# Retention and SoLU layer on one core: keys and values of later steps in blocks of half a chunk, and new orders

## The chip, the core and the metric

The kernel runs on one core of a Trainium2 chip. The core has five engines with queues of their own: PE multiplies matrices, DVE and POOL work on vectors, ACT applies functions and copies, SP only issues transfers (DMAs), which 16 DMA engines carry out. Each engine works through its instructions in the order in which the program puts them; semaphores make one wait for another. The metric is the time of one execution on the device in microseconds. A median of three runs is given, and a profile of one further execution.

## What is computed

Eight heads of a causal attention with a decay per head, for 8 sequences of 576 positions, and then a layer over all 4608 tokens:

```python
scores = scale * np.matmul(q, k.transpose(0, 1, 3, 2))
gamma = 1.0 - 2.0 ** (-5.0 - np.arange(H, dtype=np.float32))
Dmat = np.where(rel >= 0, gamma[:, None, None] ** rel[None, :, :], 0.0)
x = np.matmul(scores * Dmat[None, :, :, :], v)        # then heads side by side: 4608 x 512
...
h = x @ w_in                                           # 4608 x 1024
e = np.exp(h - h_max)
solu = h * e / (np.sum(e, axis=-1, keepdims=True) + 1e-09)
ln = (solu - mu) / np.sqrt(var + 1e-06) * g_ln
out = ln @ w_out                                       # 4608 x 512
```

All inputs and the output are 32-bit floats.

## The kernel before

**Steps.** The sequences are cut into windows of 256 positions (two a sequence) and a rest of 64; the rests of four sequences make one more window. That gives 18 windows, and each is done in two steps of four heads: 36 steps i for the attention, and 36 tiles t of 128 tokens for the layer. Steps 16, 17, 34 and 35 are the windows made of rests (here: short windows), the other 32 are full. A full window is two chunks of 128 positions. Inside a chunk all pairs of query and key are computed and masked; what lies before the chunk comes from a state (the sum of k times v so far), which is carried on.

**Interleaving.** q, k and v are loaded so that partition p holds positions 2p and 2p + 1 of the window (line 380), which makes each run in DRAM 2 x 64 floats, 512 bytes. The two positions are the two "blocks" j of 64 keys a chunk. Because the blocks interleave, each of them meets all 128 queries of its chunk, and the mask has 256 columns for a pair of blocks.

**The named operations.** A planner (`plan`, line 122) lists them, and `emit` turns each into instructions. For step i:

- ldq, ldk, ldv (line 379; 384 for short windows, as four DMAs): loads, issued by SP, each into one of five buffers of its kind
- sq, sk, cv (lines 394 and 399): scaling of q and k by powers of the decay and the cast of v to 16 bits, mostly on POOL, one tile of 128 x 512 each
- T (lines 419 and 429): transposes of q and k on PE; Te or TL (455, 457): their copy out of PSUM on ACT
- K (533): k times v for the state on PE; st (554 to 557, DVE), sm (562, POOL) and sc (571, POOL) carry the state on
- S (508): 16 score matmuls of 64 x 128 on PE; mask (540): multiplication with the mask on DVE
- I (496): the state's share of the output on PE; V (521): masked scores times v, 16 matmuls of 64 x 128 on PE; xe (576): cast of the result into xT on ACT

For tile t: M1 (587, PE), ex (595, ACT), so (605 or 610, DVE), bnA and bnB (616, DVE) or va (624, ACT), fx and rs (633, ACT; 648 and 650, POOL), L (439 or 446, PE) with Le or TL, M2 (660, PE), oe (669, ACT), and out (680, or 685 for short windows), the store, issued by SP from one of three o_sb buffers. wi, wg, wc, WM, lwi and lwo prepare the weights once, at the start; PE also multiplies zeros there where it would stand idle (846).

**Order.** Each engine's order is fixed when the program is built. For the first steps and the last ones the orders are written out by hand as lists of names (FIRST and LAST, lines 42 to 95); between them an operation's place follows from a period of 4.92 us a step and an offset of its kind (the `key`), so that every step there repeats the one before. On PE a step in the middle reads M1, M2, I, L, T, V, K, S. SP issues the loads about five steps ahead, with the store of a finished tile after every third load. `order_ops` (line 233) plays the orders through with the durations of `DUR`, which settles only how the engines' lists are merged into one program and how many multiplications of zeros are put in.

Of the kernel before, what the change touches and what calls it, by code (L numbers as in the profile page):

```python
# [9 lines left out]
FP = mybir.dt.float32  # L10
# [3 lines left out]
P = 128  # L14
# [3 lines left out]
for _b in range(0, B, 4):  # L18
# [5 lines left out]
    T=0.26, L=0.26, Tw=0.45, Lw=0.45, I=0.22, V=0.23, K=0.13, S=0.22, M1=1.73, M2=1.73, M2h=0.87, oeh=0.42, G=0.1, WM=1.73,  # L24
    TL=1.03, Te=0.58, Le=0.58, xe=0.74, ex=1.22, oe=0.69, va=1.25, wiA=0.62, wiB=0.45, wg=0.68, wgD=0.43,
    cvA=0.62, mask=1.22, st=0.58, so=1.22, soA=1.3, bnA=0.68, bnB=0.89, fx=0.2, fin=0.42, wc=0.74, wm=0.62,
    sqD=0.75, gc=0.17, cvD=0.45, sq=1.04, sk=1.04, cv=0.61, sm=0.42, sc=0.81, rs=0.69, rsB=1.0,
    ldx=0.88, ldw=1.36, out=0.65,
)
HOP, PE_OUT = 0.07, 0.2  # L30
# [4 lines left out]
ON = {'sq0': 'DVE', 'sq1': 'DVE', 'cv0': 'ACT', 'cv1': 'ACT', 'sk2': 'DVE', 'sk3': 'DVE', 'cv2': 'ACT', 'cv3': 'ACT', 'cv4': 'ACT', 'cv5': 'ACT', 'cv6': 'ACT', 'cv7': 'ACT'}  # L35
CAP = dict(
    rawq=5, rawk=5, rawv=5, q16=3, k16=4, v16=4, ev=8, s=1, ret=2, xy=1, gg=6, gt=2, s160=4, s161=9, h=1,
    e=2, solu=4, osb=3, tl=1, tlx=2, tlT=1, tlL=1, wst=5,
# [3 lines left out]
FIRST = dict(  # L42
    PE=(
# [5 lines left out]
    ),  # L49
    ACT=(  # L50
# [4 lines left out]
    ),  # L55
    DVE=(
# [5 lines left out]
    ),  # L62
    POOL=(
# [4 lines left out]
    ),  # L68
    SP=(
# [5 lines left out]
    ),  # L75
)
LAST = dict(
    PE=(
        "I34 L30 V34 S35 M1_32 I35 L31 V35 M2_28 M1_33 M2_29 M2_31 M1_34 L32 M2_30 L33 L34 M1_35 M2_32 M2_33 "
        "L35 cs M2_34 M2_35 M3"  # L80
    ),
    ACT=(
        "oe27 xe34 ex32 Le30 Le31 oe28 xe35 ex33 fx15 oe29 ex34 Le32 oe30 Le33 oe31 fx16 ex35 oe32 Le34 oe33 "
        "Le35 fx17 oe34 oe35 oz"
    ),
    DVE=(
        "so31 mask35 bnA31 so32 bnB31 bnA32 so33 bnB32 so34 bnA34 bnA33 bnB33 bnB34 cnt so35 bnA35 ci bnB35"
    ),
    POOL=(
        "rs15 rs16 rs17"  # L90
    ),
    SP=(
        "out27 out28 out29 out30 out31 out32 out33 out34 out35"
# [11 lines left out]
def ev_T(i):  # L105
    return f"Te{i}" if i < NJ + 2 else f"TL{i - 2}"


def ev_L(t):
    return f"Le{t}" if t < NJ - 4 or t + 4 > NS - 3 else f"TL{t + 4}"  # L110

# [5 lines left out]
def wide(name):  # L117

    return name[0] == "T" and int(name[1:]) < NJ + 2 or name[0] == "L" and int(name[1:]) < NJ - 4


def plan():
    ops = []
    rank = {n: x - 1e4 for lst in FIRST.values() for x, n in enumerate(lst.split())}
    rank.update({n: x + 1e4 for lst in LAST.values() for x, n in enumerate(lst.split())})

# [5 lines left out]
    for i in range(NS):  # L132
# [3 lines left out]
        n = i - 2  # L136
        for x, (nm, cs) in enumerate((("q", "sq"), ("k", "sk"), ("v", "cv"))):
            op(f"ld{nm}{i}", "SP", 0.47 if full else 1.8, [], (i - 3 - CAP["rawq"], 1.5 + x), [("raw" + nm, [f"{cs}{i}"])], DUR["ldx"])
        op(f"sq{i}", "POOL", dict(POOL="sq", DVE="sqD"), [f"ldq{i}"], (i - 3, 0.5), [("q16", [f"T{i}"])])
        op(f"sk{i}", "POOL", dict(POOL="sk", DVE="sqD"), [f"ldk{i}"], (i - 3, 1.55), [("k16", [f"T{i}", f"K{i}" if full else ""])])  # L140
# [12 lines left out]
        jn = i >= NJ + 2  # L153
        op(f"T{i}", "PE", "T" if jn else "Tw", [f"sq{i}", f"sk{i}", f"L{i - 6}" if jn else ""], (n, 0.4), [] if jn else [("tlT", [f"Te{i}"])])
        if jn:
            op(f"TL{n}", "ACT", "TL", [f"T{i}", f"L{i - 6}"], (n, 1.0), [("ev", [f"I{i}", f"S{i}", f"M2_{i - 6}"])])
        else:
            op(f"Te{i}", "ACT", "Te", [f"T{i}"], (n, 1.0), [("ev", [f"I{i}", f"S{i}"])])
        op(f"S{i}", "PE", "S", [ev_T(i)], (i - 1, 0.95), [("s", [f"mask{i}"])])
        op(f"mask{i}", "DVE", "mask", [f"S{i}"], (i - 1, 1.6), [("ret", [f"V{i}"])])  # L160
        kv = i + 2 < NS and i + 2 >= NK and WINS[(i + 2) // 2][1] < 2
        op(f"I{i}", "PE", "I", sdep + [ev_T(i)], (i - 1, 4.75), [("xy", [f"xe{i}", f"st{i + 2}" if kv else ""])])
        op(f"V{i}", "PE", "V", [f"I{i}", f"mask{i}", f"cv{i}"], (i, 0.6))
        op(f"xe{i}", "ACT", "xe", [f"V{i}", f"K{i + 2}" if kv else ""], (i, 2.0))
    for t in range(NT):
# [5 lines left out]
        op(f"so{t}", "DVE", "soA" if va else "so", [f"ex{t}"], (m, 4.56), [("solu", [f"L{t}", f"va{t}" if va else f"bnB{t}"])])  # L171
# [5 lines left out]
        if c:  # L177
# [6 lines left out]
        after = [f"Te{NJ + 1}", f"Le{t - 1}"] if t == NJ - 4 else [f"TL{NS - 3}"] if t + 4 == NS - 2 else []  # L184
        after += [f"Le{t - 2}"] if t - 2 >= NS - 6 else []
        op(f"L{t}", "PE", "Lw" if early else "L", [f"so{t}"] + after, (m + 2, 0.1),
           [("tlL" if early else "tl" if jn else "tlx", [ev_L(t)])])
        if not jn:
# [3 lines left out]
        op(f"M2_{t}", "PE", "M2h" if end else "M2", need, (t + LAG, 3.1), [("h" if end else "xy" if late(t) and t % 2 else "s", [f"oe{t}"])])  # L192
# [5 lines left out]
    for c in range(4):  # L198
        op(f"lwi{c}", "SP", 0.47, [], (-4, 0.5 + 0.1 * c), [("wst", [f"wi{c}a", f"wi{c}b"])], DUR["ldw"])
        op(f"wi{c}a", "ACT", dict(ACT="wiA", DVE="wiB"), [f"lwi{c}"], (1, 0.1 * c))  # L200
        op(f"wi{c}b", "DVE", dict(ACT="wiA", DVE="wiB"), [f"lwi{c}"], (1, 0.1 * c))
    for c in range(0, 8, 2):
        op(f"lwo{c}", "SP", 0.47, [], (-2, 0.6 + 0.1 * c), [("wst", [f"wc{c}", f"wc{c + 1}"])], DUR["ldw"])
        for x in (c, c + 1):
            op(f"wg{x}", "DVE" if x % 2 else "ACT", dict(DVE="wgD", ACT="wg"), [f"lwo{c}", "gc"], (1, 1.0 + 0.1 * x))
            op(f"wc{x}", "DVE", "wc", ["wm" if WE else "WM", f"lwo{c}"], (4, 0.1 * x))
    op("G", "PE", "G", [], (-9999, 0.0), [("h", ["gc"])])
# [15 lines left out]
def parts(name):  # L223

    if name[:2] == "lw":
        return 1
    n = int(name[3:])
    if WINS[n // 2][1] == 2:
        return 2 if name[:3] == "out" else 4
# [731 lines left out]
```

## Time and profile before

| | us |
|---|---|
| median of 3 runs | 212.61 |
| lowest, highest | 212.51, 213.25 |
| span of the profiled execution (its own time: first to last instruction) | 210.9 |

The span is what the views of the profile cover; the runs also hold what lies around it. Other groups of the page that matter for the change, with count, total and mean:

| group | count | total us | mean ns |
|---|---|---|---|
| S, PE L508, 64 x 128 | 576 | 14.8 | 218 |
| V, PE L472 from ret and v, 64 x 128 | 576 | 14.7 | 217 |
| sq, POOL L394 | 34 | 35.4 | 1042 |
| M1, PE L587 | 288 | 68.5 | 380 |
| M2, PE L660, 128 x 512 | 280 | 65.8 | 379 |

How to read it: a group's total is the time in which at least one of its instructions ran; matmuls overlap, so the mean of one is longer than the distance from one to the next. "Idle before, releaser" says how long the engine stood before these instructions and what ended it. DMA issues are not counted as busy time of an engine: to see how full SP's queue is one has to take its timeline.

### The profile page before, as it was taken

The page shows a single profiled execution, that of the slowest core. Times are in us where ns is not written, and L with a number is a line of the kernel's source. Part 1 is how long each engine was busy: PE and PEld are TensorE (multiplying, and loading weights), DVE is VectorE, ACT ScalarE, POOL GpSimd, SP SyncE. Part 2 cuts the span into 40 slices and gives each one's busy share as a digit, 9 for nine tenths or more (in the row PEclk, how much of TensorE's full clock was granted, in tenths as well). Part 3 has the DMA queues.
Part 4 walks back from the last instruction along what each step waited for, and adds up shares of the span by engine and source line. Part 5 has one row for each costly group of instructions (what it writes and reads, how often), then busy time and mean ns, then how long its engine had stood idle before and what let it go on. Part 6 is the DMA issues. An engine that isn't in the chain of part 4 may idle for free. (4 is left out here: it accounts for less than half of the span.)

```text
span 210.9 us, 10171 instructions
## 1 busy us (share of the span) xinstructions
PE 200.8 (95%) x4400; PEld 113.2 (54%) x4400; DVE 166.1 (79%) x279; ACT 141.7 (67%) x235; POOL 141.7 (67%) x240
## 2 busy tenths in 40 slices
PE   7986989999999999999999999999999999999992
PEld 2442654665566555555555555555666555554451
DVE  6565779997868898978898898889988998753760
ACT  2375787897666776776666777666767777573752
POOL 7434758999997975948787979797979792001110
PEclk9999999999999999999999999999999999999999
DMA  5999999999666559778999686776355222311224
GB/s 157 345 355 334 329 311 269 301 293 306 195 188 188 169 139 278 217 214 259 314 288 305 198 252 183 217 234 181 94 152 153 54 57 67 71 63 54 101 101 104
DMA packets 64814, 42.66 MB, mean 202 GB/s; under 512 B 3320, under 2 KB 58624, under 8 KB 64768
## 3 DMA queue, kind: packets, MB, share of 16 engines
q1 hardware_dynamic: 64528, 41.82, 68.4%
q8 instruction: 34, 0.56, 1.2%
q10 hardware_dynamic: 240, 0.18, 0.5%
q14 instruction: 12, 0.10, 0.2%
HBM read 32.55 MB, written 9.44 MB: 199 GB/s over the span
## 5 line engine op out<-in xcount | busy, mean ns | idle before, releaser
L587 PE MATMUL h_ps<-w_in,xT 128*128 128x512 f16 x288 | 68.5, 380 | 0.0
L660 PE MATMUL o_ps<-w2c,ev 128*128 128x512 f16 (+1 forms) x296 | 67.6, 373 | 0.0
L610 DVE TENSOR_TENSOR solu<-h_ps,e_sb 128x1024 f16<-128x1024 f32 x32 | 39.2, 1223 | 16.7 <-ACT e_sb L595 16.5
L595 ACT ACTIVATE e_sb<-h_ps 128x1024 f32<-128x1024 f32 x36 | 36.8, 1023 | 21.9 <-PE h_ps L587 20.4
L540 DVE TENSOR_TENSOR ret<-s_ps,masks 128x1024 f16<-128x1024 f32 x36 | 43.9, 1220 | 6.0 <-PE s_ps L508 5.4
L660 PEld LDWEIGHTS <-ev 128*128 128x128 f16 x296 | 28.7, 98 | 32.7
L616 DVE BATCH_NORM_STATS2 bs<-solu 128x6 f32<-128x512 f16 x64 | 43.6, 685 | 0.9
L587 PEld LDWEIGHTS <-xT 128*128 128x128 f16 x288 | 25.3, 98 | 29.1 <-ACT xT L576 0.8
L394 POOL TENSOR_TENSOR q<-rawq,small 128x512 f16<-128x512 f32 x34 | 35.4, 1042 | 7.3 <-DMA rawq<-in_q_dram 5.9
L669 ACT ACTIVATE o_sb<-o_ps,rs 128x512 f32<-128x512 f32 (+1 forms) x37 | 25.0, 676 | 21.8 <-PE o_ps L660 10.4
L394 POOL TENSOR_TENSOR k<-rawk,small 128x512 f16<-128x512 f32 x34 | 35.4, 1042 | 6.0 <-DMA rawk<-in_k_dram 5.9
L457 ACT COPY ev<-tl 128x1024 f32<-128x1024 f32 (+1 forms) x32 | 29.7, 932 | 4.7 <-PE tl L429 4.2
L576 ACT CAST xT<-xy 128x512 f16<-128x512 f32 x36 | 26.7, 742 | 3.0 <-PE xy L472 2.9
L571 POOL CAST sbd<-gg 64x256 f16<-64x256 f32 x64 | 25.4, 397 | 3.0
L562 POOL TENSOR_TENSOR gg<-gt,small 128x128 f32<-128x128 f32 x32 | 13.1, 409 | 16.9 <-DVE gt L557 16.5
L648 POOL TENSOR_TENSOR w<-mv,w 128x2 f32<-128x2 f32 x16 | 3.1, 194 | 27.8 <-ACT w L633 13.9
L399 POOL CAST v<-rawv 128x512 f16<-128x512 f32 x28 | 17.1, 609 | 0.2
L508 PE MATMUL s_ps<-ev 64*64 64x128 f16 x576 | 14.8, 218 | 0.3
L472 PE MATMUL xy<-ret,v 64*64 64x128 f16 x576 | 14.7, 217 | 0.0
L472 PEld LDWEIGHTS <-sbd 128*128 128x128 f16 x128 | 9.3, 98 | 9.3 <-issue 1.1
L446 PE MATMUL tl<-ident,solu 64*64 64x64 f16 x1024 | 14.2, 195 | 0.0
L846 PE MATMUL tl<-zeros 128*128 128x512 f16 x41 | 12.7, 445 | 1.3 <-DVE zeros L802 1.3
(71 smaller groups left out, 214.6 us busy)
## 6 DMA issues: line engine op xcount, KB each, us to landing
rawq<-in_q_dram SPq DMA_DIRECT2D x32, 256.0 KB, 5.1
rawk<-in_k_dram SPq DMA_DIRECT2D x32, 256.0 KB, 5.3
rawv<-in_v_dram SPq DMA_DIRECT2D x32, 256.0 KB, 5.1
out_dram<-o_sb SPq DMA_DIRECT2D x26, 256.0 KB, 3.1
out_dram<-o_sb SPq DMA_DIRECT2D x19, 128.0 KB, 2.3
wst<-in_moe_w_in_dram SPq DMA_DIRECT2D x4, 512.0 KB, 6.8
wst<-in_moe_w_out_dram SPq DMA_DIRECT2D x4, 512.0 KB, 7.1
rawq<-in_q_dram SPq DMA_DIRECT2D x16, 64.0 KB, 2.4
```

The costliest lines, as they stand in the source:

```text
L394: eng.tensor_tensor(out=t.rearrange("p j h d -> p h j d"), in0=st[i]["r" + nm], in1=g, op=ALU.mult)
L457: nc.scalar.copy(out=t[:, lo:hi].rearrange("p x (r w) -> p r x w", r=2), in_=tls[n].rearrange("p r x w -> p (r x w)").bitcast(FP).rearrang ...
L472: nc.tensor.matmul(start=(c, e) not in begun, stop=False, skip_group_check=True, **kw)
L540: nc.vector.tensor_tensor(out=d["ret"].rearrange("p e h j q -> p (e h) (j q)"), in0=d["s"].rearrange("p e h j q -> p (e h) (j q)"), in1=ma ...
L571: nc.gpsimd.tensor_copy(out=t[ee[e], :, :, ee[e]], in_=st[i]["gg"][ee[e]])
L576: nc.scalar.copy(out=xT[:, 2 * w : 2 * w + 2, 2 * hf : 2 * hf + 2].rearrange("p c h (q j) -> p c h j q", j=2), in_=xys[i][:, :, 0:256].rea ...
L587: nc.tensor.matmul(out=h_ps[:, hh], lhsT=xT[:, t, dc], rhs=w_in16[:, dc, hh], start=(dc == 0), stop=(dc == 3),)
L595: nc.scalar.activation(out=d["e"], in_=d["h"], func=ACT.Exp, accum_out=se[:, t : t + 1])
L610: nc.vector.tensor_tensor(out=d["solu"], in0=d["h"], in1=d["e"], op=ALU.mult)
L616: nc.vector.bn_stats(out=d["bs"][:, half], in_=d["solu"][:, half * 512 : half * 512 + 512])
L660: nc.tensor.matmul(out=o, lhsT=d["ev"][:, d["lo"] + c], rhs=w2c16[:, c, mm], start=(c == 0), stop=(c == 7))
L669: nc.scalar.activation(out=d["osb"][:, mm], in_=d["o", half], func=ACT.Copy, scale=ws[t // 2]["rs"][:, t % 2 : t % 2 + 1])
```

## The change

From step 14 on, in the full windows (14, 15 and 18 to 33), a block of 64 keys is no longer every second position but one half of a chunk: block 0 the positions 0 to 63, block 1 the positions 64 to 127. The queries stay as they were. Since the mask is causal, block 1 then meets only the second half of the queries, 64 of 128.

- The loads of k and v of these steps are four DMAs of 64 partitions each, with runs of 64 floats (256 bytes) in place of one DMA with runs of 512 bytes. q is loaded as before.
- k's scale takes 16 more columns of the table `small`, for the new positions.
- S and V run their 8 matmuls of block 1 over 64 columns; V reads and writes them as two strips of 32.
- A second mask of 192 columns in place of 256 is built once on POOL (mk), and the mask operation of these steps covers 4 x 192 columns in place of 4 x 256.
- The orders of all five engines are written out in full (ORDER in place of FIRST and LAST), and in the first steps many casts move: sk0, sk11 and sk14, sq2 and sq3, cv9 to DVE; sq1, sk2, sk3, cv4, cv7, wi3a and wi3b to POOL; cv8 to ACT; and more of the weights' casts between ACT and DVE. SP's list no longer follows the steps: loads of later steps stand before those of earlier ones, and stores change places (out2 before out1, out5 before out4).
- Buffers for the weights' loads are now a pool of their own at the end. Options for transposing by DMA (TX, LX), for more load buffers (R0) and for other banks at the end (OT) are in the code and switched off by their values.

```diff
+SPL = (14, 15, 16, 17, 18, 19, 20, 21, 22, 23, 24, 25, 26, 27, 28, 29, 30, 31, 32, 33, 34, 35)
...
+def split(i):
+    return i in SPL and WINS[i // 2][1] < 2
...
+        if split(i) and nm != "q":
+            for n in range(4):
+                r0 = 256 * wi + 64 * n
+                nc.sync.dma_start(
+                    out=t[64 * (n // 2) : 64 * (n // 2) + 64, :, n % 2],
+                    in_=src[b, hh, r0 : r0 + 64, :].rearrange("h p d -> p h d"),
+                )
+        elif wi < 2:
...
         for hp in range(2):
             for j in range(2):
                 for c in range(2):
                     for e in range(2):
+                        half = split(i) and j
+                        qq = slice(64 * c + 32, 64 * c + 64) if half else ee[c]
+                        oo = sz[ee[c], e, hp, 128:192] if half else sv[ee[c], e, hp, j]
                         nc.tensor.matmul(
-                            out=sv[ee[c], e, hp, j], lhsT=kT[ee[e], hp, j, ee[c]],
-                            rhs=qT[ee[e], hp, :, ee[c]], start=True, stop=True,
+                            out=oo, lhsT=kT[ee[e], hp, j, ee[c]], rhs=qT[ee[e], hp, :, qq], start=True, stop=True
                         )
...
+                        rhs, oo = d["ret"][ee[c], e, hp, j], xy[ee[e], c, 128 * hp : 128 * hp + 128]
+                        if split(i) and j:
+                            rhs = rhs[:, 0:64].rearrange("p (x q) -> p x q", x=2)
+                            oo = oo.rearrange("p (x q) -> p x q", x=2)[:, :, 32:64]
+                        mm(d["begun"], c, e, out=oo, lhsT=d["v16"][ee[c], 2 * hp + e, j], rhs=rhs)
...
+        n, m = 256, masks[:, 1 if WINS[i // 2][1] == 2 else 0]
+        if split(i):
+            n, m = 192, masks_z
...
+            in0=d["s"].rearrange("p e h j q -> p (e h) (j q)")[:, :, 0:n],
+            in1=m.unsqueeze(1).to_broadcast([P, 4, n]), op=ALU.mult,
```

The new order of SP around the places that matter, and the end of POOL's:

```text
SP    ... ldk16 ldv14 ldq12 out0 ldq13 ldq14 out2 out1 ldv16 ldk17 ldq17 ldk14 ldk15 ldv15 out3 ldk18 ldq19 out5 ldq16 out4 ...
SP    ... out17 ldk34 out18 ldv33 ldk32 ldq31 out20 ldq33 ldv34 out19 out21 ldq34 ldk33 ldv32 out22 ldv35 out23 ldk35 ldq35 out25 ...
POOL  ... rs12 sm31 sc31 cv32 sq34 sk33 cv34 sq33 sm32 sc32 sm33 sk35 rs13 sc33 cv35 sq35 rs14 rs15 rs16 rs17
```

More of the change, by code (lines that the diff above doesn't have):

```diff
@@ L136, in plan @@
         n = i - 2
+        tt = f"tx{i}" if i in TX else f"T{i}"
         for x, (nm, cs) in enumerate((("q", "sq"), ("k", "sk"), ("v", "cv"))):
[L138 to L140 removed]
+            z = split(i) and nm != "q"
+            op(f"ld{nm}{i}", "SP", 1.7 if z else 0.47 if full else 2.2, [f"wc{y}" for y in range(8)] if extra(i) else [],
+               (i - 3 - CAP["rawq"], 1.5 + x), [(("bis" if extra(i) else "raw") + nm, [f"{cs}{i}"])], DUR["ldz" if z else "ldx"])
+        op(f"sq{i}", "POOL", dict(POOL="sq", DVE="sqD"), [f"ldq{i}"], (i - 3, 0.5), [("q16", [tt])])
+        op(f"sk{i}", "POOL", dict(POOL="sk", DVE="sqD"), [f"ldk{i}"], (i - 3, 1.55), [("k16", [tt, f"K{i}" if full else ""])])
         op(f"cv{i}", "POOL", dict(POOL="cv", DVE="cvD", ACT="cvA"), [f"ldv{i}"], (i - 3, 2.6), [("v16", [f"V{i}", f"K{i}" if full else ""])])
@@ L183, in plan @@
         early = t < NJ - 4
[L184 to L188, printed above, removed]
+        if t in LX:
+            op(f"lx{t}", "SP", "lx", [f"so{t}"], (m + 2, 0.1), [("ev", [f"M2_{t}"])], DUR["ltx"])
+        lasts = [x for x in range(NT) if NJ - 4 <= x < OT and ev_L(x)[:2] == "Le"]
+        after = [f"Te{NJ + 1}", f"Le{NJ - 5}"] if t == NJ - 4 else []
+        if t in lasts:
+            after += [f"Le{t - 2}" if t - 2 in lasts else ev_T(max(i for i in range(NS) if i not in TX))]
+        if t not in LX:
+            op(f"L{t}", "PE", "Lw" if wide(f"L{t}") else "L", [f"so{t}"] + after, (m + 2, 0.1),
+               [("tlL" if early else "o2" if t >= OT else "tl" if jn else "tlx", [ev_L(t)])])
+        if ev_L(t)[:2] == "Le":
             op(f"Le{t}", "ACT", "Le", [f"L{t}"], (m + 2, 0.95), [("ev", [f"M2_{t}", "M3" if t == NT - 1 else ""])])
@@ L191, in plan @@
         need = [ev_L(t)] + [f"wc{x}" for x in range(8)] + ["cs" if t == NT - 2 else ""]
-        op(f"M2_{t}", "PE", "M2h" if end else "M2", need, (t + LAG, 3.1), [("h" if end else "xy" if late(t) and t % 2 else "s", [f"oe{t}"])])
+        if t == OT:
+            need += [ev_T(max(x for x in range(NS) if x not in TX)), ev_L(max(x for x in range(OT) if x not in LX))]
+        op(f"M2_{t}", "PE", "M2h" if end else "M2", need, (t + LAG, 3.1), [(home(t), [f"oe{t}"])])
         op(f"oe{t}", "ACT", "oeh" if end else "oe", [f"M2_{t}", f"rs{w}"], (t + LAG + 1, 0.1), [("osb", [f"out{t}"])])
@@ L223, in parts @@
 def parts(name):
-    if name[:2] == "lw":
+    if name[:2] in ("lw", "lx"):
         return 1
+    if name[:2] == "tx":
+        return 2
     n = int(name[3:])
+    if name[:2] == "ld" and split(n) and name[2] != "q":
+        return 4
     if WINS[n // 2][1] == 2:
@@ L230, in parts, with units @@
     return 2 if name[:3] == "out" and 22 <= n < 28 else 1
+def units(name):
+    if name[:3] == "out":
+        return 0.25
+    if name[:2] in ("lw", "lx", "tx"):
+        return dict(lw=0.5, lx=2.0, tx=4.0)[name[:2]]
+    return 2.0 if split(int(name[3:])) and name[2] != "q" else 1.0
 def order_ops(ops):
@@ L240, in order_ops @@
     pos = {e: 0 for e in todo}
-    quad, dma, lock, landed = False, 2.0, 0.0, []
+    quad, dma, lock, landed, held, out_at = False, 2.0, 0.0, [], 0.0, 0
     def ready(o):
-        t = max(free[o.eng], lock if o.eng == "POOL" else free["POOL"] if locks(o) else 0.0)
+        t = free[o.eng]
         for d in o.deps:
@@ L271, in order_ops @@
         start[o.name] = x
-        free[o.eng] = end = x + o.dur
+        end = x + o.dur
         if locks(o):
+            if free["POOL"] > x + 0.05:
+                end += 0.2
+                free["POOL"] += 0.18
             lock = end
+        elif o.eng == "POOL" and lock > x + 0.05:
+            end += 0.18
+        free[o.eng] = end
         if o.eng == "SP":
             end, np = x, parts(o.name)
+            u = units(o.name) / np
             for _ in range(np):
-                end = max([end + o.dur / np] + landed[-7:-6])
-                dma = max(end + 1.0, dma) + o.moved / np + (0.9 if len(landed) == 2 else 0.0)
-                landed.append(dma + 0.8)
+                begin, end = end, end + o.dur / np
+                held += u
+                while held > 5.0:
+                    held -= landed[out_at][1]
+                    end = max(end, landed[out_at][0] - 0.2)
+                    out_at += 1
+                dma = max((begin if o.name[1] == "x" else end) + 1.0, dma) + o.moved / np + (0.9 if len(landed) == 2 else 0.0)
+                landed.append((dma + 0.8, u))
             free["SP"], done[o.name] = end, dma + 0.8
@@ L339 @@
     pool("raw", CAP["rawq"])
-    for name in ("q16", "k16", "v16", "ev", "ret", "gg", "gt", "e", "solu", "osb", "wst"):
+    for name in ("q16", "k16", "v16", "ev", "ret", "gg", "gt", "e", "solu", "osb"):
         pool(name, CAP[name])
@@ L654, in mm2 @@
         d = tk[t]
-        nm = "xy" if half or late(t) and t % 2 else "s"
-        nm = "h" if t == NT - 1 and not half else nm
+        nm = "xy" if half else home(t)
         mm = slice(256 * half, 256 * half + (256 if t == NT - 1 else DM))
-        d["o", half] = o = pools[nm].tile([P, 2, 512], FP, tag=nm, name="o_ps")[:, 0, 0 : mm.stop - mm.start]
+        o = bank() if nm == "o2" else pools[nm].tile([P, 2, 512], FP, tag=nm, name="o_ps")[:, 0]
+        d["o", half] = o = o[:, 0 : mm.stop - mm.start]
         for c in range(8):
@@ L867 @@
                 emit(o)
+    if "bis" not in pools:
+        loads_w.close()
+    pool("gu", 1)
     def general(t):
```

166 lines of the change are left out of this document (101 added, 65 removed), and 69 rows, old and new, of tables (ACT, DVE, PE, POOL).

## The prediction

> **What bounds the kernel now.** I read the page first: busy shares, then the slices.
>
> ```profile
> span 210.9 us, 10171 instructions
> PE 200.8 (95%) x4400; PEld 113.2 (54%) x4400; DVE 166.1 (79%) x279; ACT 141.7 (67%) x235; POOL 141.7 (67%) x240
> PE   7986989999999999999999999999999999999992
> PEclk9999999999999999999999999999999999999999
> ```
>
> PE is the bound, at full granted clock. Next the windows of 15 us, to see where that holds (columns: length, busy PE, PEld, DVE, ACT, POOL, clock, DMA share, GB/s):
>
> ```profile
> 15.00:30.00 15.00, 13.02 (x208) 7.47 (x207) 9.72 (x19) 11.14 (x20) 8.13 (x12) 1.00 1.14 327
> 30.00:45.00 15.00, 13.60 (x244) 8.00 (x243) 14.44 (x24) 13.09 (x25) 13.60 (x21) 1.00 1.11 287
> 150.00:165.00 15.00, 15.00 (x396) 8.66 (x395) 13.48 (x22) 10.49 (x17) 12.84 (x22) 1.00 0.52 143
> ```
>
> Until about 45 us the DMA engines are full (share above 1) and PE idles 2.0 and 1.4 us; later PE has no gap. So a step costs what PE does in it, as long as its inputs are there. The PE timeline of one step (start, length, group; lengths are modelled and overlap, so I take start to start):
>
> ```profile
> 147.68 0.30 PE L429 MATMUL tl<-ident,q 64*64 64x64 f16 x16
> 147.94 0.41 PE L472 MATMUL xy<-ret,v 64*64 64x128 f16 x16
> 148.16 0.31 PE L472 MATMUL xy<-v,k 64*64 64x64 f16 x16
> 148.29 0.41 PE L508 MATMUL s_ps<-ev 64*64 64x128 f16 x16
> 148.63 1.90 PE L587 MATMUL h_ps<-w_in,xT 128*128 128x512 f16 x8
> 152.68 0.30 PE L429 MATMUL tl<-ident,q 64*64 64x64 f16 x16
> ...
> 167.46 0.30 PE L429 MATMUL tl<-ident,q 64*64 64x64 f16 x16
> ```
>
> 147.68 to 167.46 is four steps (T29 to T33), 4.94 us each; 167.46, T33, is a due time below. Last I read the DMA queue of SP, which issues every load and nearly every store, in order:
>
> ```profile
> SPq L680 <- ACT o_sb L669: 53.8, 24, 5.3
> ```
>
> 53.8 us of waiting for finished stores looks like plenty of room. The timeline of SP shows otherwise (start, length from first to last end, count):
>
> ```profile
> 57.88 0.37 SPq L680 DMA_DIRECT2D out_dram<-o_sb  x1
> 58.30 0.43 SPq L379 DMA_DIRECT2D rawv<-in_v_dram  x1
> 58.82 2.61 SPq L384 DMA_DIRECT2D rawk<-in_k_dram  x4
> 61.48 0.43 SPq L379 DMA_DIRECT2D rawv<-in_v_dram  x1
> 62.01 0.45 SPq L379 DMA_DIRECT2D rawk<-in_k_dram  x1
> 63.04 0.36 SPq L680 DMA_DIRECT2D out_dram<-o_sb  x1
> ...
> 73.98 1.82 SPq L680 DMA_DIRECT2D out_dram<-o_sb  x1
> 75.89 1.83 SPq L384 DMA_DIRECT2D rawv<-in_v_dram  x4
> ...
> 140.78 0.37 SPq L379 DMA_DIRECT2D rawv<-in_v_dram  x1
> 143.23 0.36 SPq L680 DMA_DIRECT2D out_dram<-o_sb  x1
> 143.68 2.48 SPq L384 DMA_DIRECT2D rawq<-in_q_dram  x4
> 146.26 3.15 SPq L384 DMA_DIRECT2D rawk<-in_k_dram  x4
> 149.51 1.81 SPq L384 DMA_DIRECT2D rawv<-in_v_dram  x4
> 151.42 1.15 SPq L680 DMA_DIRECT2D out_dram<-o_sb  x1
> 152.67 1.83 SPq L384 DMA_DIRECT2D rawq<-in_q_dram  x4
> 154.60 1.81 SPq L384 DMA_DIRECT2D rawk<-in_k_dram  x4
> 156.51 2.94 SPq L384 DMA_DIRECT2D rawv<-in_v_dram  x4
> 159.55 1.58 SPq L680 DMA_DIRECT2D out_dram<-o_sb  x3
> ```
>
> Three prices come out of it. Four small DMAs back to back need 1.81 to 1.83 us, and the next starts 0.1 later: 1.92 for four. A whole load starts about 0.52 before the next (61.48 to 62.01), a store 0.46 (143.23 to 143.68). And every few us one DMA stands for about a microsecond more: against 1.82 for four and 0.37 for a store, 58.82, 73.98, 143.68, 146.26, 151.42 and 156.51 show 0.8, 1.45, 0.65, 1.3, 0.8 and 1.1 too much. Where the queue has work, such a stall comes about once in a PE step. The page has one kind of traffic of that rhythm:
>
> ```profile
> q8 instruction: 34, 0.56, 1.2%
> ```
>
> 34 blocks of 16 KB, 0.94 for each of the 36 steps, 1.2% x 16 x 210.9 / 34 = 1.2 us each on one DMA engine. I read the stalls as SP standing while one engine fetches instructions; that link is inferred, the stalls are measured.
>
> **What the change removes.** In 18 steps (14, 15, 18 to 33) 8 of S's 16 matmuls and 8 of V's go from 128 to 64 columns. V to K is 0.22 us for 16 of 128 columns, K to S 0.13 for 16 of 64; half of the difference is 0.045, twice a step: 18 x 0.09 = 1.6 us of PE. The strided view that V reads and writes has no row; it could at worst keep the 128-column time, which leaves 0.8.
>
> ```profile
> L540 DVE TENSOR_TENSOR ret<-s_ps,masks 128x1024 f16<-128x1024 f32 x36 | 43.9, 1220 | 6.0 <-PE s_ps L508 5.4
> L394 POOL TENSOR_TENSOR k<-rawk,small 128x512 f16<-128x512 f32 x34 | 35.4, 1042 | 6.0 <-DMA rawk<-in_k_dram 5.9
> L399 POOL CAST v<-rawv 128x512 f16<-128x512 f32 x28 | 17.1, 609 | 0.2
> L814 POOL TENSOR_SCALAR_AFFINE_SELECT masks<-masks 128x256 f16<-128x256 f16 (+1 forms) x2 | 0.8, 412 | 0.1
> ```
>
> The mask shrinks by a quarter: 18 x 0.3 = 5.5 us of DVE, at nothing, since PE is the one without gaps and DVE is 79% busy. The casts keep their shapes.
>
> **What it adds.** Loads of k and v of those steps become four DMAs each instead of one, six more DMAs a step, 18 x 6 = 108; all of them on SP (counted in the two orders: 306 instead of 198). The mask's building adds five short POOL instructions before the first load's cast: 2.1 us by the old masks' 0.41 each, inside the 6.0 us that POOL's k casts wait for data. Casts of the first 15 steps change engines, and all orders are new. In the head the loads set the pace, so I price that at 0; bounds are -3.4 us (PE's idle time there) and about +2 (twice one cast). It hardly matters below, since the queue's late part begins at a store that PE's own progress releases.
>
> **The sum, by the queue of SP.** In the new order out2 stands ahead of out1, and behind them come all loads still needed. out2 leaves when oe2 is done (57.88; the queue is free at 58.2). From there to ldv32, the last load that T33 needs through POOL, stand 43 groups of four (35 split, 8 of the short windows), 16 whole q loads and 22 store DMAs (out1 to out21 without out2, of which out16 and out17 are two each). Bare: 43 x 1.92 = 82.6, 16 x 0.52 = 8.3, stores 18 x 0.46 + 2 x 1.0 = 10.3; together 101.2. Stalls: 109 us from 58.2 to T33 are 22.1 steps, 0.94 blocks each, 20.8; I take 0.9 us for one, near the six above (mean 1.0): 18.7. Landing of a small DMA 2.4 by this row:
>
> ```profile
> rawq<-in_q_dram SPq DMA_DIRECT2D x16, 64.0 KB, 2.4
> ```
>
> Then POOL, whose new order there is cv32 sq34 sk33 cv34 sq33: 2 x 0.61 + 3 x 1.04 = 4.3. So sq33 is ready at 58.2 + 101.2 + 18.7 + 2.4 + 4.3 = 184.8, and T33, due at 167.5, is 17.3 us late. The PE saving before T33 is lost in that wait; the 0.1 after it stays. Stores add the same lateness by another way: o_sb has three buffers, so oe22 waits till out19 has landed, and out19 stands behind 40 groups. A check from the other side: 108 DMAs at 0.48 are 51.6 us, while the queue's gaps between 58 and 161 us add up to 23.4 (24 gaps; the first and last stand between the rows 62.01 and 63.04, and 140.78 and 143.23, of that timeline); the last loads, done at 159.5 now, would end 28 us later, at 187.7, while T35 is due two steps after T33, at 177.3.
>
> Unknown is the price of a piece of 64 partitions x 4 runs of 256 bytes. Nearest is the small DMA of 32 x 4 runs, 0.48 with what lies between; the lower end is a store's 0.42 (0.36 and 0.06), the upper the 28 DMAs from 143.68 to 161.13, stalls and all, 0.62. A stall lies between half its price, 0.45, and 1.0. With 0.62 for all 210 DMAs, T33 is at 195.7, 28.2 late. With 0.42 and 0.45 together it is at 167.1, not late at all.
>
> The profile's own time is its span, 210.9; the runs' median is 212.6, 1.7 above for what lies outside the first and last instruction. 210.9 + 17.2 = 228.1 of span, 229.8 for the runs: **230 us**.
>
> **Rivals.** *One price is low.* Pieces at 0.42 with full stalls put T33 at 176.4, half stalls with full pieces at 175.4: 8 to 9 us late, 221. For it: a whole load of 512 runs is issued as fast as one of 128, so runs are not what costs; against it: 24 small DMAs at 143 to 160 us show no lower price.
>
> *The queue keeps up (not slower).* Both prices low: T33 is met, the DMAs hide as they do now, PE's 1.6 us shows: 211.0, and down to 208 if the head's idle time goes too. It decides as soon as the queue's mean is under 167.5 - 58.2 - 6.7 = 102.6 us for 210 DMAs, 0.49 each with stalls. For it: 53.8 us of idle queue. Against: most of that idle time lies where no load is left. The Trainium skill (DMA: Bandwidth & Descriptors, "Issuing engines are not separate DMA queues") says that the sequencer's time to initiate a DMA "is usually small relative to the DMA itself"; by it this rival would be the likeliest and the sum 211.0. Against it, 28 DMAs of mostly 64 KB took 17.45 us of the queue here.
>
> *The packets bind.* All-load window:
>
> ```profile
> 36.00:40.00 4.00, 3.70 (x78) 2.51 (x79) 3.68 (x7) 3.80 (x9) 3.86 (x6) 1.00 1.06 291
> ```
>
> 1.06 x 16 x 4 us over 291 GB/s x 4 us / 512 B = 2273 packets is 29.8 ns a packet. If 256 bytes cost as much as 512, a split load takes 1024 x 29.8 / 16 = 1.91 us: 35 x 1.91 + 24 x 0.95 + 20 stores x 0.95 = 108.7, T33 at 173.6, 6.1 late: 218.7. By bytes it would be 75 and fit. The Trainium skill (the same page, "Specifications") speaks for the dear end: line rate needs 512 bytes or more, smaller ones are read, modified and written. No 256-byte load runs here, so no row decides; the queue is the slower of the two either way.
>
> *The halves save nothing.* Then the queue's lateness stays what it is, and where it keeps up the time is 212.6.
>
> **Chances.** Forecast (221 to 240) 0.62; one price low 0.15; packets bind 0.06; keeps up 0.17, of which 0.04 for a saving eaten by smaller waits. Faster by over 0.5% (under 211.5) 0.13, within 0.5%, which a measurement of this kernel can't tell from no change, 0.04, slower 0.83. The range runs from 213, above the last case, to 240, the dear end: about 0.15 is left below and 0.04 above.
>
> **What would show it.** Right: SP's timeline of after without waits for o_sb from 58 to 185 us; four pieces in about 1.9 us, with stalls of a microsecond; PE gaps in most slices of the second half, ended by POOL casts that wait for DMA, or by o_sb; S and V starts closer by 0.045. Wrong: PE without gaps after 60 us, or four pieces in well under 1.7 us, or a DMA share near 1 throughout.

## The result and the profile after

| | before | after |
|---|---|---|
| median of 6 runs, us | 212.95 | 263.56 |
| lowest, highest | 212.51, 213.25 | 261.81, 264.72 |
| span of the profiled execution | 210.9 | 263.0 |

The ratio is 1.236, with a 95% interval of 1.231 to 1.240: 50.6 us slower, where 17 were forecast. Here and below a median is taken of the runs that lie within 1.5% of the fastest of the same kernel; the others are given beside it. The page of the kernel after, in the rows that answer to those of before:

```profile
span 263.0 us, 10265 instructions
PE 215.5 (82%) x4392; PEld 118.7 (45%) x4392; DVE 161.6 (61%) x283; ACT 137.7 (52%) x231; POOL 141.7 (54%) x245
PE   7799989999978698097699388469398579999993
PEclk9799999999999799779599889959779959999999
DMA  6999999956345654647543584465548352310343
q1 hardware_dynamic: 84688, 41.83, 58.2%
q8 instruction: 34, 0.56, 0.9%
L651 DVE TENSOR_TENSOR ret<-s_ps,masks_z 128x768 f16<-128x768 f32 x18 | 17.2, 954 | 37.0 <-PE s_ps L615 36.2
```

PE is no longer without gaps: from the twelfth slice (72 us) on it waits, and its granted clock, which stood at 9 in every slice before, falls to 5 to 8 tenths in one early slice and, from 85 us on, again and again. The DMA engines are full only up to the eighth slice; from the twelfth on they are busy for 3 to 6 tenths of most slices and 8 at the most, so it is not they that bind. The transposes show where the 50 us come in: T14 starts at 74.53 us (73.00 before), T20 at 117.89 (102.66), T26 at 162.41 (132.91), T33 at 219.24 (167.46); from there to the end of the span it takes 43.8 us, against 43.4. The loss grows by 2.3 to 3.2 us a step as long as split loads come, and is over with them. Up to M1 of tile 8 (63.60 us, 63.83 before) the two kernels run alike.

What the engines waited for in after (total, times, longest, in us):

```profile
POOL k L473 <- DMA rawk<-in_k_dram: 24.9, 8, 6.2
ACT o_sb L790 <- DMA out_dram<-o_sb: 19.9, 5, 5.4
POOL q L473 <- DMA rawq<-in_q_dram: 19.1, 6, 5.8
POOL v L478 <- DMA rawv<-in_v_dram: 16.6, 4, 9.3
PE s_ps L615 <- ACT o_sb L790: 13.2, 4, 4.3
PE xy L575 <- POOL v L478: 11.6, 2, 6.9
PE tl L515 <- POOL k L473: 6.3, 2, 5.6
SPq L801 <- ACT o_sb L790: 28.2, 8, 13.4
```

POOL waits for loads and ACT for stores, and PE waits for these two. The last row is SP's own waiting, 27.4 of its 28.2 us after 217 us, when no load is left. SP's timeline of after (start, length from first to last end, count):

```profile
186.97 1.97 SPq L463 DMA_DIRECT2D rawk<-in_k_dram  x4
189.04 0.38 SPq L801 DMA_DIRECT2D out_dram<-o_sb  x1
189.46 2.67 SPq L453 DMA_DIRECT2D rawv<-in_v_dram  x4
192.23 2.57 SPq L453 DMA_DIRECT2D rawk<-in_k_dram  x4
194.85 1.05 SPq L458 DMA_DIRECT2D rawq<-in_q_dram  x1
...
203.59 2.58 SPq L453 DMA_DIRECT2D rawk<-in_k_dram  x4
206.27 3.27 SPq L453 DMA_DIRECT2D rawv<-in_v_dram  x4
```

The queue issues almost without a pause, as forecast. But four pieces of the new form take 2.57 us where four small DMAs of the short windows take 1.97 here and took 1.81 before. The last row is ldv32, whose end was forecast at 178.1 us: it is at 209.54.

### The profile page after: what moved, and what is told of

Same layout as the page of the kernel before. It is cut to its first block, busy times and chain, and to the rows that moved or that the text cites. A ratio compares the mean times of both kernels' runs of the same rounds, so it can differ in the third digit from the quotient of the medians.

```text
span 263.0 us, 10265 instructions
## 1 busy us (share of the span) xinstructions
PE 215.5 (82%) x4392; PEld 118.7 (45%) x4392; DVE 161.6 (61%) x283; ACT 137.7 (52%) x231; POOL 141.7 (54%) x245
## 2 busy tenths in 40 slices
DMA packets 84974, 42.67 MB, mean 162 GB/s; under 512 B 41912, under 2 KB 78784, under 8 KB 84928
## 3 DMA queue, kind: packets, MB, share of 16 engines
q1 hardware_dynamic: 84688, 41.83, 58.2%
## 5 line engine op out<-in xcount | busy, mean ns | idle before, releaser
L708 PE MATMUL h_ps<-w_in,xT 128*128 128x512 f16 x288 | 78.9, 424 | 0.3 <-DVE solu L726 0.3
L781 PE MATMUL o_ps<-w2c,ev 128*128 128x512 f16 (+1 forms) x296 | 69.1, 379 | 0.0
L473 POOL TENSOR_TENSOR q<-rawq,small 128x512 f16<-128x512 f32 x33 | 34.3, 1041 | 19.5 <-DMA rawq<-in_q_dram 19.1
L708 PEld LDWEIGHTS <-xT 128*128 128x128 f16 x288 | 28.0, 106 | 35.5 <-issue 12.0
L651 DVE TENSOR_TENSOR ret<-s_ps,masks_z 128x768 f16<-128x768 f32 x18 | 17.2, 954 | 37.0 <-PE s_ps L615 36.2
L615 PE MATMUL s_ps<-ev 64*64 64x128 f16 (+1 forms) x576 | 15.5, 229 | 13.5 <-ACT o_sb L790 13.2
L651 DVE TENSOR_TENSOR ret<-s_ps,masks 128x1024 f16<-128x1024 f32 x18 | 21.9, 1218 | 6.2 <-PE s_ps L615 5.9
L769 POOL TENSOR_TENSOR w<-mv,w 128x2 f32<-128x2 f32 x16 | 3.1, 194 | 28.2 <-DVE mv L739 24.3
L615 PEld LDWEIGHTS <-ev 64*64 64x64 f16 x576 | 11.2, 117 | 14.8 <-issue 13.8
L575 PE MATMUL xy<-v,k 64*64 64x64 f16 x384 | 8.1, 201 | 11.6 <-POOL v L478 11.6
L575 PE MATMUL xy<-ev,sbd 128*128 128x128 f16 (+1 forms) x128 | 13.2, 214 | 4.5 <-POOL sbd L692 2.4
```

The lines of the kernel that those rows point to most:

```text
L473: eng.tensor_tensor(out=t.rearrange("p j h d -> p h j d"), in0=st[i]["r" + nm], in1=g, op=ALU.mult)
L615: nc.tensor.matmul(out=oo, lhsT=kT[ee[e], hp, j, ee[c]], rhs=qT[ee[e], hp, :, qq], start=True, stop=True)
L651: nc.vector.tensor_tensor(out=d["ret"].rearrange("p e h j q -> p (e h) (j q)")[:, :, 0:n], in0=d["s"].rearrange("p e h j q -> p (e h) (j q ...
L708: nc.tensor.matmul(out=h_ps[:, hh], lhsT=xT[:, t, dc], rhs=w_in16[:, dc, hh], start=(dc == 0), stop=(dc == 3),)
L781: nc.tensor.matmul(out=o, lhsT=d["ev"][:, d["lo"] + c], rhs=w2c16[:, c, mm], start=(c == 0), stop=(c == 7))
```

## The experiments

Eleven kernels were run. All times are compared with runs of the kernel before on the same chip (213.2 to 213.4 us).

### Orders, halves and pieces apart

The new orders alone: `SPL = ()` in the changed kernel.

> The new orders alone: no step is split, every load of k and v is one DMA again, the matmuls and the mask keep their old size. Theory (SP's queue is the bound, through the number and the price of its DMAs): 198 DMAs as before, so SP keeps up and the time is 211 to 215 us. Rival (the new orders themselves cost the time: out2 ahead of out1, loads of later steps ahead of earlier ones): well above 225 us, with waits for o_sb and for loads as in the changed kernel.

Measured: 215.22 us, ratio 1.010 (1.004 to 1.017), a little above the range expected. The orders cost some 2 us, where the prediction had 0, and leave 48 of the 50 us to the rest.

The halved matmuls and the short mask in the new orders, with whole loads:

```diff
-        if split(i) and nm != "q":
+        if False:
             for n in range(4):
...
-        o = (78 if split(i) and nm == "k" else base + (16 if WINS[w][1] == 2 else 0)) + 8 * hf
+        o = (base + (16 if WINS[w][1] == 2 else 0)) + 8 * hf
```

> The halved matmuls and mask with the new orders, but every load one DMA of the old positions and k scaled as before, so that the second block's scores belong to other keys than the mask assumes: the computation of the values differs, the work on PE and DVE is that of the change. Theory: 1.0 to 1.8 us under the kernel with the new orders alone (18 steps x 0.09), 209 to 213 us. Rival (half-width matmuls with strips save nothing or cost): equal to the orders alone within 0.5 us, or slower.

Measured: 212.72 us, ratio 0.998 (0.993 to 1.002), no different from before and 2.5 us (1.2%) below the new orders alone; two of its ten runs took 216.0 us, and with them it is 1.7 us below on the mean. The halves do save something near the 1.6 us that were forecast, but the runs of one kernel lie 2 to 3 us apart and don't fix the size.

The pieces alone, in the orders and with the computation of before:

```diff
-        if wi < 2:
+        if wi < 2 and i >= 14 and nm != "q":
+            for n in range(4):
+                r0 = 256 * wi + 128 * (n // 2)
+                nc.sync.dma_start(
+                    out=t[64 * (n // 2) : 64 * (n // 2) + 64, :, n % 2],
+                    in_=src[b, hh, r0 : r0 + 128, :].rearrange("h (p j) d -> p h j d", j=2)[:, :, n % 2],
+                )
+        elif wi < 2:
```

> Old orders, old matmuls and mask; only the loads of k and v from step 14 on are four DMAs of 64 partitions with runs of 256 bytes, at the old positions. Theory: SP is as late as in the changed kernel, since 10 DMAs a step with eight of them at 0.65 us and a stall of one microsecond are 7.3 us against 4.9 of PE: 250 to 268 us. Rival (new orders): 212 to 216 us.

Measured: 262.89 us in one run. The pieces alone make the kernel as slow as the whole change.

### The price of one DMA, by its form

The kernel before, with the v loads of steps 20 to 33 in four forms by turns (`form = (i - 20) % 4`): two of 64 partitions with runs of 512 bytes (L383), four of 32 partitions with 512 (L386), two of 128 partitions with 256 (L389), and four of 64 partitions with 256 (L393), the form of the change.

> The kernel before, with the loads of v in steps 20 to 33 in four forms in turn: two DMAs of 64 partitions with 512-byte runs, four of 32 partitions with 512-byte runs, two of 128 partitions with 256-byte runs, four of 64 partitions with 256-byte runs. It measures the price of one DMA on SP's queue. Known so far: 0.43 us for 32 partitions with 512-byte runs, 0.61 for 64 partitions with 256-byte runs. If the run's length sets the price, the two forms with 256 bytes take 0.6 and the others 0.43; if 64 partitions set it, the two forms with 64 partitions take 0.6 and the others 0.43; if both add up, 64 partitions with 512 bytes and 128 partitions with 256 bytes lie between. The time is 212 to 217 us, since only 1.7 DMAs a step are added.

The rows of the tile rawv in this kernel (line, engine, count, shortest, median and longest ns, first and last start):

```profile
L386 SPq DMA_DIRECT2D rawv<-in_v_dram x16: 422/428/904, 93.3 to 148.4; - x16
L393 SPq DMA_DIRECT2D rawv<-in_v_dram x12: 600/618/1495, 100.0 to 138.6; - x12
L383 SPq DMA_DIRECT2D rawv<-in_v_dram x8: 607/634/1548, 89.8 to 143.5; - x8
L389 SPq DMA_DIRECT2D rawv<-in_v_dram x6: 368/501/531, 97.7 to 131.5; - x6
```

The length of a run does not matter: 64 partitions cost 0.63 us with 512 bytes and 0.62 with 256. 32 partitions cost 0.43, and 128 partitions, with twice the runs of a piece, only 0.50. It is the 64 partitions that are dear, which no count of runs or bytes explains; why they are dearer than both 32 and 128, no run here shows. The kernel as a whole took 214.07 us in its one run.

### Number, packets or form

Three runs set the candidates against each other. Four DMAs of 32 partitions instead of 64, all else as in the kernel with the pieces alone:

```diff
-        if wi < 2:
+        if wi < 2 and i >= 14 and nm != "q":
+            x = src[b, hh, 256 * wi : 256 * wi + 256, :].rearrange("h (p j) d -> p h j d", j=2)
+            for n in range(4):
+                nc.sync.dma_start(out=t[32 * n : 32 * n + 32], in_=x[32 * n : 32 * n + 32])
```

> The kernel before, its orders and its computation, with the k and v of the 18 full steps from 14 on loaded as four DMAs each of 32 partitions with runs of 512 bytes: as many DMAs as the change issues, but of the form that the prediction took its price from (0.43 us each in the run of the four forms, against 0.62 us for 64 partitions). If the price is set by the partitions and the rest of the prediction's sum is sound, four take about 1.8 us, the queue is late by some 20 us at step 33, and the kernel takes 225 to 240 us. If it is the number of DMAs that costs, whatever their form: about 262 us. If packets of 256 bytes are what binds: 213 us, as there are none here.

Measured: 240.69 us, ratio 1.127 (1.118 to 1.136), just above the range expected. With the same number of DMAs it is 22 us faster than the pieces alone, so the number alone is not it. Nor are packets of 256 bytes alone, of which the k and v loads here have none: it is still 27 us slower than before.

Two DMAs of 128 partitions with runs of 256 bytes (`out=t[:, :, n], in_=x[:, :, n]`):

> The kernel before, with the same k and v loaded as two DMAs each of 128 partitions with runs of 256 bytes: the same number of packets, of the same size, as the change makes, in half as many DMAs at about 0.5 us each. SyncE's queue then has some 3.0 us a step and a stall of about 1 us in a step of 4.7 us: it keeps up, 212 to 215 us. If packets of 256 bytes were what binds, it would be as slow as the pieces alone: about 263 us.

Measured: 212.92 us in the profiled execution; the only other run took 219.98 us, which is still 43 us below the pieces alone. The page of the first:

```profile
span 211.2 us, 10223 instructions
DMA packets 83822, 42.66 MB, mean 202 GB/s; under 512 B 40760, under 2 KB 77632, under 8 KB 83776
```

There are 40760 small packets, against 41912 in after, and T33 starts at 167.42 us (167.46 before): the packets do not bind.

The changed kernel itself, with its four DMAs in the form of 32 partitions, for which the prediction's sum was made:

> The changed kernel, orders and halved computation included, with nothing else altered than the form of its four DMAs: 32 partitions with runs of 512 bytes instead of 64 partitions with runs of 256. The keys then stand in the places of before, so the output differs from the reference's: the work is the same. This is the kernel for which the prediction made its sum, with DMAs of the very form that it took its price from (0.43 us each by the run of the four forms, 0.48 in its sum). If only that price failed in the prediction, the time is 224 to 236 us around its 230, and the stall at blocks of instructions goes on. If other steps of its sum were wrong as well (the stalls, the landing, the stores), it lies beyond: 240 to 250 us, as the same DMAs in the orders of before took 240.7.

Measured: 238.8 and 242.6 us in its two runs, the one between the two answers and the other in the second; the profile is of the slower one. Tiles rawk and rawv of that kernel:

```profile
L453 SPq DMA_DIRECT2D rawk<-in_k_dram x72: 312/430/2156, 68.2 to 186.5; - x72
L453 SPq DMA_DIRECT2D rawv<-in_v_dram x72: 311/430/2213, 51.1 to 189.3; - x72
```

and of the kernel after:

```profile
L453 SPq DMA_DIRECT2D rawk<-in_k_dram x72: 595/614/1507, 67.7 to 205.6; - x72
L453 SPq DMA_DIRECT2D rawv<-in_v_dram x72: 595/615/1853, 50.6 to 208.9; - x72
```

With the price that the prediction took, 21 to 25 of the missing 33.5 us are gone, and 9 to 13 stay. So the price of a piece is the large error, and it is not the only one.

### The halves in the old orders, and loads by window

The halves in the orders of before, whole loads, the mask as a constant by one DMA:

> The kernel before, in its own orders and with whole loads, with the halved matmuls and the shorter mask from step 14 on; the mask comes as a constant by one DMA. Its keys stand in the places of before, so its output differs from the reference's: what is timed is the work alone. By the new orders' cost of 2 us and the halves' saving of 1.6 to 2.1 us as measured so far: 210.5 to 211.5 us, 0.7 to 1% below the kernel before. If the saving came only from the new orders fitting the halves, the time stays at 212.6.

Measured: 212.38 us, ratio 0.995 (0.992 to 0.998): 0.5% less than before on the same chip (1.0 us), where 0.7 to 1% was expected. The PE timeline of a step there, beside that of before in the prediction:

```profile
147.78 0.30 PE L441 MATMUL tl<-ident,q 64*64 64x64 f16 x16
147.91 0.31 PE L441 MATMUL tl<-ident,k 64*64 64x64 f16 x16
148.03 0.36 PE L484 MATMUL xy<-ret,v 64*64 64x128 f16 x16
148.21 0.31 PE L484 MATMUL xy<-v,k 64*64 64x64 f16 x16
148.34 0.36 PE L524 MATMUL s_ps<-ev 64*64 64x128 f16 x16
148.63 1.90 PE L607 MATMUL h_ps<-w_in,xT 128*128 128x512 f16 x8
150.37 1.89 PE L680 MATMUL o_ps<-w2c,ev 128*128 128x512 f16 x8
...
152.68 0.30 PE L441 MATMUL tl<-ident,q 64*64 64x64 f16 x16
```

From V to K it is 0.18 us (0.22 before), from S to M1 0.29 (0.34): 0.04 and 0.05, the forecast 0.045 each. The step is 4.90 us, where the same one took 5.00 before. Why only 1.0 us of 18 x 0.09 shows in the time of the kernel is open.

That half per cent is what a better way to load could win. One DMA can bring the 64 partitions of all 8 heads, for both steps of a window, which halves the number of DMAs (the buffers and SP's order change with it):

```diff
...
+            for n in range(4):
+                r0 = 256 * wi + 64 * n
+                nc.sync.dma_start(
+                    out=cur[w, nm][64 * (n // 2) : 64 * (n // 2) + 64, :, n % 2],
+                    in_=src[b, :, r0 : r0 + 64, :].rearrange("h p d -> p h d"),
+                )
...
```

> All of the computation of the change from step 14 on, in the orders of before, but k and v loaded for the two steps of a window at once: one DMA of 64 partitions with 8 heads for each half of a chunk, so four DMAs for two steps where the change has eight, in buffers of a window's size. If the partitions set the price of a DMA (0.62 us), SyncE has about 7 us of issue and 1.9 us of stalls in two steps of 9.4 us: it keeps up, and the halves' saving comes out, 210.5 to 212 us. If the number of runs sets it (512 runs here, twice as many), a DMA costs about 1.2 us, two steps need some 13.5 us, and the kernel takes about 245 us.

Measured: 219.3 us, ratio 1.028 (1.023 to 1.034), between the two answers. Two of its six runs took 222.4 and 223.8 us, and the profile is of the first of these. The DMAs did keep the price of 64 partitions, with twice the runs:

```profile
L415 SPq DMA_DIRECT2D rawk<-in_k_dram x36: 595/640/2165, 50.5 to 148.6; - x36
```

but the queue, full, put the stores behind two groups of loads. ACT's timeline shows the price of one such place (in brackets the idle time before and what ended it):

```profile
115.22 0.69 ACT L719 ACTIVATE o_sb<-o_ps,rs 128x512 f32<-128x512 f32 x1 [3.32 <-DMA out_dram<-o_sb]
```

The second version loads q and the short windows by window too and puts each store between two loads:

> As the kernel that loads k and v by window, which took 219.5 us with its DMAs at 0.64 us, mended where its profile showed the loss: SyncE was issuing without a pause from 85 to 171 us, and a store that stood behind two groups of loads held ScalarE's o_sb for 3.3 us at 112 us and for 4.3 us at 171 us. Here q and the short windows are loaded by window too (one DMA for q in two steps, twelve for the two short steps instead of twenty-four), and every store stands between the loads, at most one group ahead of it. SyncE then has some 8.5 us in two steps of 9.7 us, and 5 us less at each pair of short steps. If the queue's occupancy was the cause: no wait of o_sb for a store over 1 us between 100 and 170 us, and 211 to 213 us, so the halves' saving of about 1 us comes out. If it was something else in the loads by window (their landing, or the packets of 256 bytes), it stays at 217 us or more.

Measured: 214.4 us, ratio 1.004 (1.000 to 1.008): 5 us better than the first version and no different from before, above the 211 to 213 expected. Three of its eleven runs took 216.8 to 219.9 us. The wait it was made against is down to one of 1.3 us, where none over 1 us was expected:

```profile
ACT o_sb L718 <- DMA out_dram<-o_sb: 1.3, 1, 1.3
```

The third lets ACT issue twelve of the stores (`(nc.scalar if 10 <= t < 22 else nc.sync).dma_start(...)`):

> As the second kernel that loads by window (214.6 us, no different from before), with the stores of tokens 10 to 21 issued by ScalarE right behind their o_sb and no longer by SyncE. That takes some 1 us of 8.9 us in two steps off SyncE's queue and puts a store on ScalarE, which is busy 66% of its time. If what kept the halves' saving from coming out there was the queue near its limit: 212 to 213.3 us, just below before. If ScalarE's issue of 0.4 us or more a store delays its evictions: 214.5 to 217 us.

Measured: 213.55 us, ratio 1.003 (1.000 to 1.005), between the two answers. So no version was found that beats the kernel before: the loads by window take the loss away, but the halves' half per cent does not come out with them. Why not was not settled. The profile can't tell: it is of the fastest of twelve runs (212.24 us, span 210.5), and the fastest run of before on that chip is as fast (212.17, span 210.5).

## Why the prediction was wrong

The mechanism was right, its size was not: 230 us were forecast, with a range from 213 to 240, and 263.56 measured. Here is the sum of the prediction against SP's records, from the queue's being free behind out2 to the end of ldv32. A DMA's bare price is the mean of those within 0.2 us of their kind's median, with the usual gap to the next one; what is above is counted as stall, and gaps over 0.12 us as waits.

| us | forecast | after | after with 32 partitions |
|---|---|---|---|
| queue free at (behind out2) | 58.2 | 57.6 | 58.2 |
| 35 split groups of four | 67.2 | 93.4 | 67.4 |
| 8 groups of short windows | 15.4 | 15.7 | 15.4 |
| 16 q loads | 8.3 | 9.4 | 8.3 |
| stores (22 DMAs) | 10.3 | 12.5 | 11.2 |
| stalls | 18.7 | 19.0 | 25.8 |
| waits of the queue | 0 | 1.9 | 3.5 |
| end of ldv32 to T33 | 6.7 | 9.7 | 6.9 |
| T33 starts at | 184.8 | 219.2 | 196.6 |

**The price of a piece: the step that failed.** The prediction wrote of a piece of 64 partitions: "Nearest is the small DMA of 32 x 4 runs, 0.48 with what lies between". The piece took 0.667 with what lies between (93.4 / 140), 26.2 of the 34.4 us that T33 came later than forecast. A nearer row stood in the profile of before. The two-piece stores are of 64 partitions, and at 159.55 us three store DMAs, one of 128 partitions and two of 64, needed 1.58 us. The prediction priced such a pair at 1.0 us among its stores and did not carry that price over to the pieces. Singled out, in the tile out_dram of before (L685 issues stores of 64 partitions only):

```profile
L685 SPq DMA_DIRECT2D out_dram<-o_sb x7: 466/551/757, 128.4 to 207.4; - x7
```

These stores took 0.55 us for 64 partitions with one run each (0.47 to 0.59 without a stall, the longer ones right behind another store), when a store of 128 took 0.36. The prediction compared by the number of runs, said itself that "runs are not what costs", and did not look for what does. Its upper bound of 0.62, stalls included, fell below the 0.667 without stalls, so the range was too low by construction. What stands right behind a piece takes longer too: a store of 128 partitions right behind a piece took 0.55 us, and 0.38 behind a piece of 32 partitions. That is most of what stores and q loads took above the forecast, 2.2 and 1.1 us.

**The stalls.** 18.7 us of stalls were forecast and 19.0 measured: this term held. The link to the instruction blocks, called inferred there, is supported: over thirteen profiles (before, after and the eleven experiments), of 297 DMA issues after 48 us that took over 0.95 us, 274 overlap one of the 16-KB packets of the queue q8 by more than 0.05 us; of 2095 that took up to 0.72 us, only 161 do. It stays a coincidence in time, as no kernel with fewer instructions was tried. The Trainium skill (Runtime: NRT & Kernel Launch, "Instruction fetch mechanics") says that instructions come in blocks of 16 KiB by a DMA queue of the sequencer's own; the 34 packets of 0.56 MB agree. The same section of the Trainium skill calls the cost of crossing a block mostly hidden; the stalls here, 23 of 0.8 us on average in that sum of after, speak against it if the link holds. With pieces of 32 partitions the stalls were longer, 25.8 us. With the waits (3.5) and the stores (0.9 more than forecast) that is what starts T33 at 196.6 instead of 184.8 there. It comes from the slower of that kernel's two runs; in the orders of before the same comparison gives 21.0 us of stalls with 32 partitions and 17.0 with the pieces. Why is open.

**The last step to T33.** POOL's work was taken as what stands between ldv32 and T33. PE's timeline in after (in brackets the wait):

```profile
207.21 0.37 PE L615 MATMUL s_ps<-ev 64*64 64x128 f16 x16
212.27 0.43 PE L575 MATMUL xy<-v,k 64*64 64x64 f16 x16 [4.70 <-POOL v L478]
212.63 3.60 PE L708 MATMUL h_ps<-w_in,xT 128*128 128x512 f16 x8
216.02 2.72 PE L781 MATMUL o_ps<-w2c,ev 128*128 128x512 f16 x8
218.58 0.28 PE L575 MATMUL xy<-ev,sbd 128*128 128x128 f16 x2
218.79 0.45 PE L534 MATMUL tl<-ident,solu 64*64 64x64 f16 x32
219.06 0.35 PE L575 MATMUL xy<-ret,v 64*64 64x128 f16 x16
219.24 0.30 PE L515 MATMUL tl<-ident,q 64*64 64x64 f16 x16
```

It is K32, the row that waits, that ldv32 holds up through cv32, and M1 of one tile and M2 of another stand between it and T33 in PE's order. After the wait they ran at a lower granted clock (0.50 from 212 to 216 us, 0.74 from there to 219.3): 3.60 and 2.72 us instead of 1.90 and 1.89, 2.5 us of the 3.0 that this step is off. So the path of this step was wrong as well, though most of what it cost is the clock's. In the kernel with 32 partitions M1 and M2 took 1.90 and 1.89 us here and the step 6.9; that the 6.7 added up from POOL's casts is so near is chance.

**The halves.** 0.045 twice a step was right by the rows above; of the 1.6 us that it adds up to, the kernel with whole loads in the orders of before shows 1.0. In after the saving is lost in PE's waits, as said. The shorter mask saves 18 x 0.27 us of DVE; that it saves nothing of the time was not tried apart.

**The new orders.** Priced at 0 with a bound of about +2, they cost 2 us, though not in the head: with the orders alone T14 starts at 72.94 us (73.00 before), T33 at 168.88 (167.46). The bound held, as far as the interval (0.4 to 1.7%) tells, the place did not.

**The rivals.** "One price is low" and "the queue keeps up" are out: the price was above the dear end, not below. The queue does keep up with two DMAs of 128 partitions, at 212.9 us. "The packets bind" is out by the same run, and a packet of 256 bytes took 18 ns on average in after, one of 512 took 30, so the 256 bytes did not cost as much as the 512 either. The rule of the Trainium skill that line rate needs 512 bytes (DMA: Bandwidth & Descriptors, "Specifications") did not decide here. Nor did the sentence of the Trainium skill (the same page, "Issuing engines are not separate DMA queues") that initiating a DMA is usually small beside the DMA: SP was the bound while the DMA engines had room. Another page has this case: the Trainium skill (Perfetto Trace Analysis, "What 'DMA-bound' means") counts an issuing engine's track solid with DMA slices as a bound of its own, and after shows just that from 58 to 210 us.

**What would show it.** No wait for o_sb over 0.4 us in SP's timeline, stalls of about a microsecond, PE gaps ended by POOL's casts and by o_sb, S and V starts closer: all are there. "Four pieces in about 1.9 us" is the one that is wrong: they took 2.57. Of the side sums, 108 DMAs at 0.48 us are 51.8 us and not 51.6, which changes nothing.

## What to carry to other kernels

SP's queue had a price per DMA here that the form set and not the bytes. Before more DMAs are put on it, look for a row of the same number of partitions in the trace, or time one form of each by turns in a running kernel, which one run did here. Compare what the queue must issue with the time until its last load is due, stalls included, and see what stands behind the loads: a late store stops a compute engine as surely as a late load. A saving of 0.09 us a step on the bound engine can't pay for six more DMAs a step once they fill the queue: ten DMAs, eight of them at 0.67 us, and a stall of 0.8 come to some 7 us, by estimate from these prices, where a step had 4.94.

## What the runs showed of the hardware

- A load issued by SP right behind one of its kind took 0.43 us with 32 partitions, 0.61 to 0.64 with 64 and about 0.50 with 128 (medians); runs of 256 or 512 bytes, and 4 or 8 of them a partition, made a difference of 0.03 us at most at 64.
- PE's granted clock, 1.00 in every window of 15 us from 15 to 195 us before, was 0.77 from 120 to 135 us and from 165 to 195 in after, where PE waited often. Windows of after (length, busy PE, PEld, DVE, ACT, POOL, clock, DMA share, GB/s):

```profile
120.00:135.00 15.00, 10.52 (x209) 5.34 (x211) 7.04 (x13) 5.58 (x10) 8.83 (x14) 0.77 0.65 178
165.00:195.00 30.00, 20.19 (x400) 10.61 (x399) 13.96 (x26) 11.45 (x19) 15.19 (x27) 0.77 0.54 136
```

Most of it should cost nothing, since SP's queue, which PE waits for, itself waited for only 1.9 us; that is argued, no run shows it apart. On the way to T33, where M1 and M2 followed a wait of 4.7 us at up to twice their length, it counted.
